# Writing the PSUM banks down per task and moving twenty-one tasks in a planned attention and Hyena kernel

## The chip, the cores and the metric

The kernel runs on one core of one Trainium2 chip. The metric is the device time of one execution in microseconds. The kernel before was timed in three runs: 375.69, 372.85 and 372.73 us, a median of 372.85 us. The profile shows one further execution, whose instructions span 370.8 us.

## The reference

The program computes an attention with an extra one in the denominator of the softmax, and feeds it to a gated long convolution:

```python
scores = scale * q @ k.T                      # 8 batches, 12 heads, 448 x 448, head size 64
e = np.exp(scores - m)                        # m: the row maximum
attn = e / (e.sum(-1) + np.exp(-m) + 1e-9)
x = (attn @ v)                                # gathered to 8 x 448 x 768
proj = x @ w_proj                             # 768 -> x1, x2, x3 of 768 each
x2_conv = irfft(rfft(x2, axis=1) * rfft(filter, axis=0), axis=1)
out = (x1 * x2_conv * x3) @ w_out
```

Everything is float32 at the edges; the kernel works in bf16 between them and accumulates in float32.

## The kernel before

**Two parts.** `attention(i)` (L934) handles one pair of heads, i = 0 to 47, six to a batch. `dense(b)` (L1099) handles the projection, the convolution as matrix products and the output product of batch b, 0 to 7. Attention of a later batch is interleaved with the dense part of an earlier one, so that TensorE (PE) has dense matmuls to run while ScalarE (ACT) works through the exponentials.

**Tasks.** No engine's order is left to a compiler. Each step is handed to `Plan.add` (L83) as a task: its engine, an assumed cost, what it needs, what it makes, which buffers it takes and gives back. `Plan.run` (L91) walks through the tasks in a planned time of its own and emits them. Since `plan.ORDER` (L455) is filled, each engine runs its tasks strictly in the order of that list's numbers: an engine looks only at the first task of its queue (L227) and waits for it. `plan.FLIP` (L456) lists the tasks that run on the other of two engines, ACT or VectorE (DVE), than the one they are written with.

**PSUM.** Eight banks are shared by three kinds of tile: pairs of banks for scores (`sc`) and for attention outputs (`op`), single banks (`hy`) for everything else. `spots` (L171) hands them out while the plan runs: to each tile a bank that is free at that planned time, by rules of preference. A tile's first matmul therefore waits on the chip for whoever empties the previous tile of the same bank.

The tasks that this document speaks of, by the names used here:

- S(i, t): four score matmuls of head pair i into an `sc` pair, 64x64 tiles of the array (L947, L952); then an exponential on ACT (L966).
- ER(i): the part of `e @ v` from the short rest of the rows, 64x64 tiles, 16 matmuls (L977); a pair of head pairs shares one `op` pair of banks, and the even one's ER is the first to write it. V(i, u): the main part, 12 matmuls of 128x128 (L997). Then `norm` on DVE, three instructions (L1010 to L1012), gives the `op` pair back.
- G(b, dt, part): six matmuls of the gate projections (L1273). Part 0 is copied to `x1` (L486 on ACT or L488 on DVE); part 1 is multiplied with it into `g` on DVE (L1288).
- PS(b, dt): six matmuls of the convolved projection (L1175), copied to a staging tile (L486 or L488), then turned by a DMA transpose into `x2` (`turn2`, L1188). Z(b, ...) are the matmuls on `x2` (L1223).
- I(b, dt): four matmuls back from the spectrum (L1319), copied to `cr`, added and subtracted into `cw` (L1335, L1337) and `cv` (L1346), multiplied with `g` into `y` (L1361: `yT` and, for the last 64 rows, `yR`).
- O(b, st, ch): the output product from `y` (L1091); the first three of a batch come as four matmuls and then two. It is copied into `osb`, of which there are three (L394), and stored by SP (L1406). A copy into `osb` waits until the store that used the buffer three before has landed.
- Loads: SP issues loads of q and k (L727, L747), of the rests (L509) and the DMA transposes into `qT`, `kT` (L694, L705), `xT` (L1056) and `x2` (L1188). GpSimd (POOL) issues the loads of v (L754) and casts q, k, v and the rests (L733, L759, L771, L514). Both run in their own fixed order.

Of the kernel before, what the change touches and what calls it, by code (L numbers as in the profile page):

```python
# [41 lines left out]
class Plan:  # L42
# [17 lines left out]
    FLIP = ()  # L60
    FETCH = (4.6, 256, 150)
# [14 lines left out]
    def __init__(self, rings):  # L76
        self.size = rings
        self.tasks = []
        self.banks = {}
        self.kept = []  # L80
        self.open = []

    def add(self, eng, cost, want, emit, need=(), make=(), take=(), give=(), dma=0.0, run=256, n=1, after=0.0, begun=(), late=0.0, turn=False, part=None, keep=False, port=False, mode=None, alt=None, mm=None):  # L83
        if alt:
            own = (eng, cost)
            (eng, cost), alt = (alt, own) if len(self.tasks) in self.FLIP else (own, alt)
            emit = lambda f=emit, e=eng: f(e)
        want = self.ORDER[len(self.tasks)] if self.ORDER else want + self.SHIFT.get(part, 0.0)
        self.tasks.append((want, len(self.tasks), eng, cost, emit, need, make, take, give, dma, after, run, n, begun, late, turn, keep, port or eng == "POOL" and not dma, mode or ("full" if eng == "PE" and not keep else None), alt, 2 * (mm or max(1, round(cost / 0.17)) if eng == "PE" and cost else 0)))

    def run(self):  # L91
# [79 lines left out]
        def spots(t):  # L171

            found, count = {}, {}
            for r, tok in t[7]:
                if r not in self.CAP or (r, tok) in self.banks:
                    continue
                count[r] = count.get(r, 0) + 1
                have = sum(1 for o in self.banks if o[0] == r and gone.get(o, 1e9) > now + 1e-9)
                if have + count[r] > self.CAP[r]:
                    return None  # L180
                busy = {i for got in found.values() for i in got}
                open_ = [i for i in range(self.NBANKS) if i not in busy and until[i] <= now + 1e-9]
                if r in self.PAIRS:
                    pairs = [(max(until[i], until[i + 1]), i) for i in open_ if i % 2 == 0 and i + 1 in open_]
                    if not pairs:
                        return None
                    i = min(pairs)[1]
                    found[(r, tok)] = (i, i + 1)
                else:
                    if not open_:  # L190
                        return None
                    found[(r, tok)] = (min(open_, key=lambda i: (self.MATE and i ^ 1 in open_, i < self.LOW, until[i], i)),)
            return found

        def ready(t):
            e = t[2]
            if not self.ORDER and t[10] > now + 1e-9:
                return False
            for k in t[5]:
                if made.get(k, 0):  # L200
                    return False
                at, by = when.get(k, (0.0, e))
                if at + (self.LAT[by] if by != e else 0.0) > now + 1e-9:
                    return False
            if e in queues and t[9]:
                out = sum(h[2][12] for h in queues[e]) + sum(x > now + 1e-9 for x in landed[e])
                if out + t[12] > self.OPEN:
                    return False
            if spots(t) is None:
                return False  # L210
            new = {}
            for r, tok in t[7]:
                if (r, tok) in holds or r in self.CAP:
                    continue
                h = held[r]
                i = len(h) + new.get(r, 0) - self.size[r]
                new[r] = new.get(r, 0) + 1
                if i >= 0 and gone.get((r, h[i]), 1e9) > now + 1e-9:
                    return False
            return True  # L220

        while any(queue.values()):
            moved = False
            for e in queue:
# [9 lines left out]
                for key, at in spots(t).items():  # L234
                    self.banks[key] = at
                    for j in at:
                        until[j] = 1e9
# [9 lines left out]
                if t[20]:  # L247
                    after, block, shift = self.FETCH
                    wait, cost = 0.0, end - now
                    edge = (fed - shift) // block * block + block + shift  # L250
                    while edge <= fed + t[20]:
                        at = now + cost * (edge - fed) / t[20] + wait
# [35 lines left out]
        for i, (_, t) in enumerate(order):  # L288
            if i in full:
                self.fill(*full[i])  # L290
            if t[16]:
                mine = {x for key in t[8] for x in self.banks.get(key, ())}
# [46 lines left out]
def kernel(  # L339
# [101 lines left out]
    def couple(c):  # L441
# [6 lines left out]
    plan = Plan(  # L448
        {
            "e": NE, "er": 2 * NER, "k0": 2, "q0": 2, "u": 1, "w": 1, "xf": 1,  # L450
            "x2": 1, "x2s": 1, "x2h": 1, "xs": 2, "t0": 2, "t1": 2, "yh": 1, "g": 1, "x1": 2, "cr": 2, "cw": 1, "cv": 2, "yT": 1, "yR": 1,
            "os": 3,
        }
    )
# [61 lines left out]
    def staged(b):  # L516
# [3 lines left out]
        for hp in range(NHP):  # L520
# [6 lines left out]
            for n, (name, x, at, size) in enumerate(parts):  # L527
# [29 lines left out]
                if alone:  # L557
                    add("ACT" if first else "SP", 0.52 if first else 0.5, -21.0 if first else want + 0.1 * n, load,
                        make=[("s" + name, g)], after=hold, dma=0.95 if name == "q" else 0.71, run=50)
                elif hp % 2 == 0:  # L560
                    need = [("cv", g - 6), ("cv", g - 5)] if name == "v" and c >= 3 else []
                    if name != "v" and c >= 4:
                        need = [("c" + w, c - 4) for w in "kq"]
                    add("POOL", 0.73, want + 0.1 * n, load, need=need, make=[(made, g), (made, g + 1)], after=hold, dma=1.05 if name == "q" else 1.0, run=45)
                if hp == 0 and name != "q":
                    add("SP", 2.6, want + (0.05 if name == "k" else SLOT[0] + 0.05) if b == 0 else want - RE1 + 0.1 * n,
                        lambda name=name: rests_load(name, b),
                        need=[("cr" + name, b - 1)] if b else (), make=[("r" + name, b)],
                        dma=1.25, run=22, begun=[("ir", b)], n=4)
# [1055 lines left out]
    with (  # L1625
# [6 lines left out]
        for b in range(n_batches):  # L1632
            W["yT", b], W["yR", b // 2] = y, yr
            stable(b)
            plan = Plan(plan.size)
# [9 lines left out]
    with tc.manual_schedule(engines={E.PE, E.Pool, E.DVE, E.Activation, E.SP}):  # L1645
        plan = main
# [31 lines left out]
```

## Time and profile before

| | us |
|---|---|
| three timed runs | 375.69, 372.85, 372.73 |
| median of the runs | 372.85 |
| profiled execution, first to last instruction | 370.8 |
| median less that span | 2.05 |
| PE busy in the span | 356.4 (96%) |
| DVE busy | 274.8 (74%) |
| ACT busy | 237.5 (64%) |
| POOL busy | 127.6 (34%) |

The profiled execution has no timed total of its own, only its span; the 2.05 us between the span and the median are what lies around the instructions. A row of the timeline reads: start in us, length in us, engine, source line, operation, output and inputs, shapes, count, and in brackets how long the engine had been idle before it and what ended that. Matmuls overlap each other, so the distance between two starts says what a group costs, and its length says a little more. PE's weight loads have an engine name of their own, PEld. Rows are matched with tasks by the order of each engine's instructions.

### The profile page before, as it was taken

Reading aid. Unit: us, or ns where it says so; the run is one execution under the profiler, and the core shown is the slowest. Engines: PE = TensorE matmul, PEld = TensorE weight load, DVE = VectorE, ACT = ScalarE, POOL = GpSimd, SP = SyncE. Lnnn points to the kernel's source line nnn. Section 1 sums busy time; section 2 is a strip of 40 time slices with the busy share of each in tenths; the row PEclk is TensorE's granted clock in tenths of the full one; section 3 lists DMA queues with packets and bytes.
Section 4 is the critical chain, followed back from the end, with each engine's and each line's share of the span. In section 5 each row is a group of like instructions: output and inputs, shape, how many; then the busy total and the mean of one; then the engine's idle time right before and its main releaser. Section 6 shows DMA issues by size and latency. Waiting matters only on the chain. (4 is left out here: it accounts for less than half of the span.)

```text
span 370.8 us, 10707 instructions
## 1 busy us (share of the span) xinstructions
PE 356.4 (96%) x4300; PEld 211.8 (57%) x4300; DVE 274.8 (74%) x674; ACT 237.5 (64%) x379; POOL 127.6 (34%) x278
## 2 busy tenths in 40 slices
PE   7989999999999979999999999999999999999995
PEld 7666675554555545565555646665565655555552
DVE  5468659982789726897579977689459898779970
ACT  4999876756767548567565657867776561334343
POOL 9984251444625274265537523313100100000000
PEclk9999999999999999999999999999999999999999
DMA  9999999988999999999998799995830074125035
GB/s 169 194 191 204 207 207 205 206 169 160 168 242 156 229 214 208 235 242 192 206 182 202 166 245 192 262 208 122 171 72 1 7 196 89 42 45 170 4 129 172
DMA packets 133958, 61.93 MB, mean 167 GB/s; under 512 B 105165, under 2 KB 130704, under 8 KB 133904
## 3 DMA queue, kind: packets, MB, share of 16 engines
q1 hardware_dynamic: 111552, 48.71, 61.6%
q0 software_dynamic: 22112, 12.26, 25.4%
q8 instruction: 34, 0.56, 0.6%
q10 hardware_dynamic: 240, 0.23, 0.2%
q14 instruction: 20, 0.16, 0.2%
HBM read 43.86 MB, written 11.01 MB: 148 GB/s over the span
## 5 line engine op out<-in xcount | busy, mean ns | idle before, releaser
L966 ACT ACTIVATE e<-psum 128x896 bf16<-128x896 f32 x144 | 126.6, 920 | 40.8 <-PE psum L947 37.3
L1273 PE MATMUL psum<-xT,wproj_bf 128*128 128x448 bf16 x576 | 121.7, 353 | 0.1
L1273 PEld LDWEIGHTS <-wproj_bf 128*128 128x128 bf16 x576 | 53.4, 98 | 47.7 <-issue 5.0
L1091 PE MATMUL psum<-wout_bf,yT 128*128 128x384 bf16 x288 | 54.7, 326 | 0.8 <-DVE g L1288 0.4
L1175 PE MATMUL psum<-xf,wproj_bf 128*128 128x452 bf16 x252 | 53.9, 357 | 0.0
L947 PE MATMUL psum<-qT,kT 64*64 64x448 bf16 x576 | 45.4, 359 | 2.5 <-DVE g L1288 0.7
L997 PEld LDWEIGHTS <-e 128*128 128x128 bf16 x1152 | 42.0, 98 | 9.6 <-issue 5.2
L997 PE MATMUL psum<-vn,e 128*128 128x65 bf16 x1152 | 46.8, 194 | 0.0
L733 POOL CAST nat<-nat 112x512 bf16<-112x512 f32 x36 | 25.4, 708 | 44.7 <-DMA nat<-in_q_dram 41.8
L1241 DVE TENSOR_TENSOR t<-xs,hrs 113x768 bf16<-113x768 bf16 (+1 forms) x64 | 36.4, 578 | 2.9 <-ACT xs L486 2.3
L1288 DVE TENSOR_TENSOR g<-x,psum 128x448 bf16<-128x448 bf16 x48 | 29.2, 616 | 12.1 <-PE psum L1273 10.9
L1091 PEld LDWEIGHTS <-yT 128*128 128x128 bf16 x288 | 26.6, 98 | 19.9 <-issue 1.8
L1175 PEld LDWEIGHTS <-wproj_bf 128*128 128x128 bf16 x252 | 23.2, 96 | 22.2 <-issue 1.1
L486 ACT CAST x<-psum 128x448 bf16<-128x448 f32 (+1 forms) x39 | 20.4, 529 | 22.6 <-PE psum L1273 14.5
L759 POOL CAST nat<-nat 128x384 bf16<-128x384 f32 x36 | 21.5, 598 | 32.2 <-DMA nat<-in_k_dram 31.9
L486 ACT COPY osb<-psum 128x384 f32<-128x384 f32 x39 | 18.2, 486 | 20.1 <-PE psum L1091 15.9
L486 ACT CAST xs<-psum 113x384 bf16<-113x384 f32 (+1 forms) x41 | 19.2, 482 | 15.1 <-PE psum L1223 14.1
L1012 DVE TENSOR_TENSOR xb<-psum,den 128x896 bf16<-128x896 f32 x24 | 26.2, 1091 | 0.8
L486 ACT CAST cr<-psum 128x452 bf16<-128x452 f32 x35 | 18.0, 539 | 11.5 <-PE psum L1319 11.0
L947 PEld LDWEIGHTS <-kT 64*64 64x64 bf16 x576 | 15.6, 105 | 17.1 <-issue 12.9
L966 ACT ACTIVATE er<-psum 128x896 bf16<-128x896 f32 x24 | 22.2, 926 | 4.3 <-PE psum L952 3.5
L987 POOL MEMSET sinks<- 1x1 bf16 x18 | 1.6, 91 | 65.6 <-PE psum L977 65.6
(143 smaller groups left out, 501.3 us busy)
## 6 DMA issues: line engine op xcount, KB each, us to landing
nat<-in_q_dram SPq DMA_DIRECT2D x37, 224.0 KB, 3.8
out_dram<-osb SPq DMA_DIRECT2D x21, 384.0 KB, 3.5
nat<-in_k_dram SPq DMA_DIRECT2D x38, 192.0 KB, 3.9
nat<-in_v_dram POOLq DMA_DIRECT2D x15, 192.0 KB, 6.3
wproj_bf<-in_moe_w_proj_dram POOLq DMA_DIRECT2D x2, 1152.0 KB, 18.1
out_dram<-osb SPq DMA_DIRECT2D x12, 192.0 KB, 2.7
ks<-in_v_dram POOLq DMA_DIRECT2D x9, 192.0 KB, 4.9
rests<-in_k_dram SPq DMA_DIRECT2D x32, 48.0 KB, 4.3
```

The costliest lines, as they stand in the source:

```text
L486: nc.scalar.copy(to, of)
L733: lambda hp=hp, qsrc=qsrc: nc.gpsimd.tensor_copy(qn[:, hp].rearrange("p j (u d) -> p u j d", u=2), qsrc.rearrange("p (u j d) -> p u j d", ...
L759: lambda hp=hp, sv=sv: nc.gpsimd.tensor_copy(kn[:, hp // 2, 3 * (hp % 2) + 1 : 3 * (hp % 2) + 4].rearrange("p j (u d) -> p u j d", u=2), sv),
L947: nc.tensor.matmul(sc[r, u, 0:S], kT[b % 2][c, hp // 2, 3 * turned + t, r], qT[b % 2][c, hp, :])
L966: nc.scalar.activation(to, of, AF.Exp, scale=SCALE)
L997: nc.tensor.matmul(out_bank(u)[:, n + 3 * turned, :], P["e"][1 + t][:, o : o + 128], vn[b % 2][:, hp, 4 * u + t, :], start=False, stop=tur ...
L1012: nc.vector.tensor_tensor(W["xb", b][:, hp // 2].rearrange("p s (u d) -> p u s d", u=2), op[:, :, :, 0:DH], rec[:].unsqueeze(3).to_broadca ...
L1091: nc.tensor.matmul(ops[:n, :DCH], y[:, dt, 0:n], wout_bf[:, dt, ch * DCH : (ch + 1) * DCH], start=(dt == 0), stop=(dt == NDT - 1),)
L1175: nc.tensor.matmul(pps, wproj_bf[:, kt, D + dt * 128 : D + (dt + 1) * 128], W["xf", b][:, :, kt, 0:FQ], start=(kt == 0), stop=(kt == NDT - 1),
L1241: nc.vector.tensor_tensor(t[:K], L["xs", par, ch][:K], h, op=ALU.mult)
L1273: nc.tensor.matmul(p[:, :S], wproj_bf[:, kt, 2 * part * D + dt * 128 : 2 * part * D + (dt + 1) * 128], xT()[:, kt, 0:S], start=(kt == 0), ...
L1288: nc.vector.tensor_tensor(g[:, dt, :], L["x1", dt], p[:, :S], op=ALU.mult)
```

## The change

The planner gets a list `BANK`. The first time that a task takes a PSUM tile, the tile gets the next number of the list as its bank (or as the first bank of its pair), and `spots` may use no other:

```diff
+    BANK = ()
...
+        self.mine = {}
...
+        for r, tok in take:
+            if r in self.CAP and self.BANK:
+                self.mine.setdefault((r, tok), self.BANK[len(self.mine)])
...
-                if r in self.PAIRS:
+                mine = self.mine.get((r, tok))
+                if mine is not None:
+                    at = (mine, mine + 1) if r in self.PAIRS else (mine,)
+                    if any(i not in open_ for i in at):
+                        return None
+                    found[(r, tok)] = at
+                elif r in self.PAIRS:
...
-    plan.ORDER = (9, 0, 6, 1370, 8, 10, 1, 5, 13, 18, 20,
...
+    plan.ORDER = (9, 2, 6, 1370, 8, 10, 1, 5, 13, 18, 20,
...
+    plan.BANK = (4, 4, 6, 4, 4, 6, 5, 4, 4, 7, 5, 4, 5, 4,
...
```

The list has 535 numbers, one for each tile. Tile by tile they are the banks that the planner hands out in the kernel before. So no tile changes its bank; what the list does is to hold the banks where they are while tasks move.

`ORDER` is written anew, and many of its 2033 numbers differ, but read engine by engine only eighteen tasks stand elsewhere in their queue. From `FLIP` the tasks 1027 and 1573 go and 1635 comes in, which puts three copies on ACT instead of DVE. These are the twenty-one:

| engine | task | moved | now ahead of |
|---|---|---|---|
| PE | V(6, 0) | 1 earlier | the first four matmuls of G(0, 0, 0) |
| PE | V(17, 0) and V(17, 1) | 2 earlier each | S(18, 1), S(18, 2) |
| PE | G(2, 2, 0) | 8 earlier | S(20, 0), S(21, 1), the ends of O(1, 1, 0) and O(1, 0, 1), PS(2, 2), S(21, 2), S(21, 3), ER(20) |
| PE | V(26, 0) | 2 earlier | both parts of O(2, 1, 0) |
| DVE | `ft` scaling (L870) | 1 earlier | the cast of the first q |
| DVE | `g` of G(0, 3, 1) | 3 earlier | `cw`, `cw`, `cv` of the first pair of I |
| DVE | `y` of batch 0, first third | 8 earlier | among others a `norm` |
| DVE | a minimum of denominators (L1046) | 12 later | nothing; it waits longer |
| DVE | a sum into `yh`, batch 1 (L1247) | 3 earlier | `g` of G(1, 1, 1) and two others |
| DVE | `g` of G(1, 5, 1) | 1 earlier | the second `cw` of batch 1 |
| DVE | `yR` of batch 1, second third | 2 earlier | another `yR` and the `norm` of 18, 19 |
| DVE | `g` of G(2, 0, 1) | 1 earlier | the `norm` of 18, 19 |
| SP | transpose into kT(16) | 2 earlier | that of qT(16), a load of q |
| SP | transpose into kT(17) | 2 earlier | that of qT(17), the first `x2` of batch 1 |
| SP | load of k(23) | 2 earlier | loads of k(22), q(22) |
| POOL | half of the key rests of batch 4 (L514) | 7 earlier | casts of q(24), k(25), q(25), k(26), k(24), the issue of a load of v(26), v(27), the other half |
| POOL | cast of k(26) | 3 later | nothing |
| DVE to ACT | `x1` of G(0, 2, 0) | | |
| DVE to ACT | `cr` of I(4, 2) | | |
| DVE to ACT | staging copy of PS(5, 1) | | |

(Positions of DVE count without the copies that leave it.) No instruction is added or taken away, apart from single filler matmuls on zeros (L1566) that the planner puts into gaps of the first 40 us and whose number it works out anew.

More of the change, by code (lines that the diff above doesn't have):

```diff
@@ new lines @@
+    plan.BANK = (4, 4, 6, 4, 4, 6, 5, 4, 4, 7, 5, 4, 5, 4, 5, 5, 4, 1, 0, 5, 4, 0, 4, 1, 6, 2, 0, 2, 6, 0, 2, 0, 0, 6, 6, 6, 2, 4, 2, 2, 6, 0, 4, 4, 4, 6, 0, 0, 0, 2, 4, 0, 6, 2, 6, 2, 2, 6, 2, 0, 6, 0, 0, 4, 6, 6, 4, 0, 2, 0, 2, 4, 6, 6, 0, 2, 2, 2, 4, 0, 6, 6, 6, 0, 0, 0, 0, 4, 0, 4, 6, 4, 4, 6, 2, 4, 4, 6, 6, 6, 0, 6, 2, 4, 0, 4, 6, 4, 4, 2, 2, 4, 6, 0, 4, 0, 4, 0, 2, 2, 6, 4, 2, 4, 4, 4, 0, 4, 6, 2, 2, 0, 0, 4, 2, 2, 0, 4, 2, 6, 4, 6, 6, 2, 4, 2, 4, 2, 6, 2, 0, 2, 6, 4, 6, 4, 0, 4, 2, 2, 4, 0, 2, 6, 2, 6, 0, 4, 2, 6, 0, 0, 2, 6, 0, 4, 0, 6, 4, 4, 4, 6, 6, 4, 2, 2, 0, 0, 6, 0, 4, 6, 4, 4, 2, 6, 0, 2, 2, 6, 0, 6, 0, 4, 4, 4, 2, 2, 0, 0, 6, 2, 0, 2, 6, 2, 2, 6, 0, 6, 7, 6, 1, 0, 3, 2, 5, 3, 2, 4, 4, 4, 7, 5, 2, 3, 5, 1, 4, 0, 4, 5, 1, 4, 5, 4, 0, 5, 1, 0, 2, 4, 4, 5, 5, 3, 4, 6, 2, 2, 3, 3, 2, 2, 3, 2, 3, 4, 2, 3, 0, 1, 5, 7, 3, 2, 0, 1, 3, 7, 0, 1, 1, 6, 0, 2, 6, 7, 6, 7, 3, 2, 3, 7, 6, 6, 4, 0, 0, 1, 3, 7, 3, 7, 2, 0, 1, 1, 3, 0, 2, 1, 0, 3, 2, 7, 7, 1, 4, 1, 0, 4, 7, 4, 6, 6, 1, 2, 6, 5, 5, 1, 6, 2, 5, 0, 1, 4, 4, 7, 5, 0, 5, 3, 4, 4, 5, 7, 0, 7, 0, 1, 6, 0, 3, 1, 2, 3, 7, 5, 0, 4, 1, 2, 1, 4, 3, 0, 0, 2, 3, 4, 1, 3, 6, 7, 0, 2, 0, 1, 5, 3, 6, 5, 4, 7, 0, 7, 0, 0, 1, 1, 0, 7, 5, 4, 0, 6, 1, 3, 6, 2, 2, 7, 6, 2, 2, 7, 3, 7, 3, 7, 5, 6, 6, 2, 0, 4, 5, 1, 0, 6, 2, 1, 0, 6, 4, 7, 6, 2, 1, 6, 7, 2, 4, 5, 0, 3, 3, 7, 6, 4, 7, 3, 5, 2, 7, 5, 7, 6, 1, 1, 4, 4, 6, 7, 2, 5, 4, 5, 4, 4, 4, 5, 5, 5, 4, 7, 6, 5, 4, 6, 5, 4, 4, 4, 6, 5, 6, 6, 7, 4, 5, 3, 0, 4, 7, 2, 4, 5, 4, 2, 6, 7, 7, 7, 5, 6, 5, 5, 4, 4, 7, 7, 0, 5, 7, 5, 6, 5, 7, 0, 5, 4, 4, 3, 6, 6, 5, 4, 5, 3, 1, 7, 6, 7, 6, 4, 5, 7, 7, 6, 7, 6, 4)
@@ new lines @@
+    plan.FLIP = (30, 49, 71, 87, 94, 98, 376, 378, 380, 438, 464, 971, 975, 977, 979, 985, 993, 1018, 1029, 1074, 1105, 1110, 1114, 1125, 1133, 1143, 1173, 1199, 1207, 1211, 1221, 1240, 1253, 1256, 1260, 1270, 1276, 1286, 1294, 1320, 1322, 1351, 1353, 1368, 1381, 1383, 1388, 1398, 1400, 1428, 1436, 1472, 1476, 1481, 1505, 1514, 1518, 1523, 1533, 1541, 1585, 1599, 1604, 1611, 1618, 1635, 1640, 1644, 1649, 1651, 1675, 1679, 1689, 1693, 1703, 1746, 1751, 1753, 1772, 1777, 1782, 1796, 1802, 1810, 1814, 1824, 1838, 1856, 1900, 1905, 1907, 1909, 1916, 1932, 1940, 1944, 1954, 1994)
```

3 lines of the change are left out of this document (1 added, 2 removed).

## The prediction

> **What bounds the kernel now.** I read the page first, then the table by stretches, then the timeline wherever PE stood still.
>
> ```profile
> span 370.8 us, 10707 instructions
> PE 356.4 (96%) x4300; PEld 211.8 (57%) x4300; DVE 274.8 (74%) x674; ACT 237.5 (64%) x379; POOL 127.6 (34%) x278
> PEclk9999999999999999999999999999999999999999
> 100.00:120.00 20.00, 18.72 (x257) 10.70 (x255) 18.46 (x45) 14.96 (x23) 8.23 (x19) 1.00 1.23 190
> 120.00:140.00 20.00, 17.47 (x207) 10.00 (x206) 10.54 (x26) 10.38 (x15) 10.60 (x23) 1.00 1.06 216
> 300.00:320.00 20.00, 20.00 (x190) 11.26 (x191) 16.39 (x44) 7.04 (x11) 0.09 (x1) 1.00 0.44 111
> ```
>
> PE is the bound, at full clock. It idles 370.8 - 356.4 = 14.4 us in all, and a change that adds and removes no matmul can win nothing but that. The idle time is not spread out: the stretch 120 to 140 alone holds 20 - 17.47 = 2.5 us, and late stretches such as 300 to 320 hold none. So each move is worth the idle time of PE that lies where the task now stands, as long as nothing later gives it back.
>
> The largest stop, and its cause, in the timeline around it and in the view of the tile `osb`:
>
> ```profile
> 123.62 0.76 POOL L754 DMA_DIRECT2D ks<-in_v_dram  x1
> 124.72 0.41 SPq L1406 DMA_DIRECT2D out_dram<-osb  x1
> 125.97 1.09 DVE L1012 TENSOR_TENSOR xb<-psum,den 128x896 bf16<-128x896 f32 x1
> 127.02 0.38 PE L952 MATMUL psum<-qT,kT 64*64 64x448 bf16 x4
> 127.23 0.36 PE L947 MATMUL psum<-qT,kT 64*64 64x448 bf16 x4
> 127.23 0.62 DVE L1288 TENSOR_TENSOR g<-x,psum 128x448 bf16<-128x448 bf16 x1
> 129.45 0.57 PE L947 MATMUL psum<-qT,kT 64*64 64x448 bf16 x8
> 131.66 1.02 DVE L488 COPY osb<-psum 128x384 f32<-128x384 f32 x2 [3.81 <-DMA out_dram<-osb]
> 132.27 0.19 PE L977 MATMUL psum<-vn,er 64*64 64x65 bf16 x1 [2.25 <-DVE osb L488]
> 132.98 1.31 PE L1273 MATMUL psum<-xT,wproj_bf 128*128 128x448 bf16 x6
> 134.13 0.54 PE L997 MATMUL psum<-vn,e 128*128 128x65 bf16 x12
> DMA to landing us min/median/max: 4.3/5.6/6.8
> ```
>
> Two output copies want `osb` buffers, and the store that still reads one of them, issued at 124.72, lands only at about 131.6 (6.8 us, the longer of the two stores in that view). Until then DVE stands, the two banks under the copies stay full, and ER(20), whose `op` pair is those banks, holds PE. Then comes G(2, 2, 0) at 132.98, which needs none of this.
>
> **The change part by part.** The list of banks first: it names the banks that the tiles have now, so alone it moves nothing, and I cost it at 0.
>
> *G(2, 2, 0) into the stop.* One gate costs 134.13 - 132.98 = 1.15 us of PE. It now runs at about 127, ahead of the score groups. Its bank is emptied by the `g` of G(2, 0, 1), which is moved ahead of the `norm` with it: 1.09 us of `norm` and its two small instructions no longer precede it, so it ends near 126.5, and G can start at 126.9 without waiting. Behind it S(20, 0) to S(21, 3) come 1.15 us later. Does that hurt? The scores cost 0.21 us a group (127.02 to 127.23), so the last would have ended at 129.45 + 0.42 = 129.87; now it ends at 131.0, still before the copies free ER(20) at 132.27. The exponentials behind them shift, but the stop has room. So the stop shrinks by the whole gate: **-1.15**. If the store lands when ER(20) is next anyway, the cover is gone and the move is worth 0. What stays of the stop: 132.98 - 129.87 - 0.23 (ER with its change of tile, below) - 1.15 = 1.73 us.
>
> *V(26, 0) ahead of O(2, 1, 0).*
>
> ```profile
> 176.82 1.33 PE L1175 MATMUL psum<-xf,wproj_bf 128*128 128x452 bf16 x6
> 178.52 1.14 PE L1091 MATMUL psum<-wout_bf,yT 128*128 128x384 bf16 x6 [0.36 <-DVE g L1288]
> 179.49 0.54 PE L997 MATMUL psum<-vn,e 128*128 128x65 bf16 x12
> 179.96 0.38 PE L947 MATMUL psum<-qT,kT 64*64 64x448 bf16 x4
> ```
>
> The output product waits for a bank that DVE empties. A group like the one at 176.82 takes about 1.15, so PE could have gone on near 178.0 and lost 0.5. V takes 179.96 - 179.49 = 0.47 less a change of tile of 0.09, that is 0.38, and its operands are long there: **-0.38**, 0 if DVE is on time.
>
> *Two copies to ACT, `cr` of I(4, 2) and the staging copy of PS(5, 1).*
>
> ```profile
> 254.05 0.63 DVE L488 CAST nat<-psum 128x452 bf16<-128x452 f32 x1
> 255.21 0.92 ACT L966 ACTIVATE e<-psum 128x896 bf16<-128x896 f32 x1 [1.31 <-PE psum L947]
> 257.57 0.50 PE L1091 MATMUL psum<-wout_bf,yT 128*128 128x384 bf16 x2
> 258.66 0.62 DVE L1288 TENSOR_TENSOR g<-x,psum 128x448 bf16<-128x448 bf16 x1
> 258.78 0.30 PE L977 MATMUL psum<-vn,er 64*64 64x65 bf16 x14
> 259.33 0.38 PE L947 MATMUL psum<-qT,kT 64*64 64x448 bf16 x4 [0.25 <-DVE g L1288]
> ```
>
> DVE works without a pause up to the `g` at 258.66, whose bank the scores at 259.33 take. ER before them costs some 0.15, so 0.4 is lost there, and 0.15 more at 257.57. With the 0.63 of the copy at 254.05 off DVE, and the same again a little earlier, both go; ACT has 1.31 us free at 253.9. I take **-0.5**, between 0 and -0.55.
>
> *What lies ahead of 132 and does not count.* The other moves sit at or before the stop:
>
> ```profile
> 63.76 0.37 PE L1319 MATMUL psum<-bt,yh 113*128 113x113 bf16 x4 [0.41 <-DVE x L488]
> 76.86 0.82 PE L1091 MATMUL psum<-wout_bf,yT 128*128 128x384 bf16 x4 [0.31 <-DVE yT L1361]
> 102.98 0.53 PE L1223 MATMUL psum<-x,ft 113*113 113x384 bf16 x2 [0.81 <-DMA x<-ldm]
> 115.91 0.38 PE L947 MATMUL psum<-qT,kT 64*64 64x448 bf16 x4 [0.47 <-DVE g L1288]
> ```
>
> `x1` of G(0, 2, 0) on ACT frees the bank that I(0, 1) waits for (0.41); `y` and `g` of batch 0 come earlier and end the wait at 76.86 (0.31 and some before it); the earlier `g` of G(1, 5, 1) ends that at 115.91 (0.47). The scaling of `ft`, the `yh` sum and V(6, 0) act the same way on smaller waits, the late minimum only yields its place. Together about 1.2 to 2. But behind them PE meets two DMA landings, at 102.98 and 132.27. If those hold their time, PE only arrives earlier and waits longer: **0**.
>
> V(17, 0) and V(17, 1) ahead of S(18, 1) part two runs of 64x64 tiles that touched, two changes of tile more.
>
> ```profile
> 112.26 0.36 PE L952 MATMUL psum<-qT,kT 64*64 64x448 bf16 x4
> 112.56 2.44 PE L1273 MATMUL psum<-xT,wproj_bf 128*128 128x448 bf16 x12
> ```
>
> From the start of the last score group to the next 128x128 matmul pass 0.30 instead of the 0.21 of a group: 0.09 a change, 0.18 for the pair, hidden in the stop at 132; without that cover, +0.18. The Trainium skill, TensorEngine Tiling (Array Packing), section Tiling Modes, says that a change of tiling mode drains TensorE, which speaks against this move; the trace agrees that it costs something, and if a drain cost a matmul's whole 0.36 us the pair would come to +0.7 and still lie under the stop.
>
> *The queues.* On SP three entries pass two others each and no entry is added. On POOL the key rests of batch 4 now wait, ahead of seven others, for transposes that read the same tile:
>
> ```profile
> 121.55 1.93 SPq L705 DMA_TRANSPOSE kT<-nat  x1
> 122.72 0.77 POOL L733 CAST nat<-nat 112x512 bf16<-112x512 f32 x1 [6.66 <-DMA nat<-in_q_dram]
> 131.88 0.50 POOL L514 CAST nat<-rests 64x384 bf16<-64x384 f32 x1
> 133.90 1.69 SPq L1188 DMA_TRANSPOSE x<-ldm  x1
> 143.77 0.65 PE L1223 MATMUL psum<-x,ft 113*113 113x384 bf16 x3
> q0 software_dynamic: 530, 0.20, 14.0%
> ```
>
> The cast of q(24) waits some 3 us longer (an estimate: the transpose at 121.55 with the 4 us or so that other DMAs take here), and the v load of 123.62 behind it goes out at about 127. The rest of POOL's list is bound by later landings and ends no later than 131.88 + 0.50. PE wants the first result that hangs on it, the `x2` at 133.90, only at 143.77. Cost **0**.
>
> Sum: -1.15 - 0.38 - 0.5 = -2.0. On the profile's own span that is 370.8 - 2.0 = 368.8; with the 2.05 us between span and median, 372.85 - 2.0 = **370.8 us**. The unknown term is the store's landing, x: every us that it moves moves the end as far, since PE works almost without pause behind it. Earlier it can win the 1.73 left of the stop; later it costs without limit, and 2 us is what separates the two ends of the landings above (4.3 and 6.8) roughly. I take 0, as the queue ahead of the store has the same entries.
>
> **The rivals.**
>
> *A: the store comes earlier.* The v load leaves the time before the landing. In the window 118 to 133 the POOL queue took 14.0% of the engines' time, 2.1 of 15 us. If half or more of this goes behind the store, x is -1 to -1.73: 369.1 to 369.8. Against it: the load still overlaps the last 4 us. The Trainium skill, DMA: Bandwidth & Descriptors, section Issuing engines are not separate DMA queues, says that DMAs of all issuers run on the same 16 engines and interleave. By that rule the load did delay the store. The trace agrees as far as it goes: the store needed 6.8 us while that load was under way, the other store of the view 4.3.
>
> *B: the gain is hidden.* Either the timed runs do not have the stop at 132 (then the gate wins nothing: -0.38 - 0.5 = -0.9, 372.0), or ACT, now with 0.54 us more in two places, delays exponentials: 372 to 373. For it: one profiled execution only. Against it: two timed runs agree within 0.12 us.
>
> *C: slower, the store comes later.* Place: the DVE copy at 131.66. Price: 1 us per us. It decides from 2.0 us later, beyond 133.6. For it: some of SP's entries ahead of the store change places, and a store's landing took anything from 4.3 to 6.8. Then 373 to 375; a stop of more than 5.7 us extra would be needed for 1%. Against it: the transposes are the same number, and none is bigger.
>
> *D: it does not do what it says.* The list holds the banks as they are; were one of the moved tiles to wait for a bank that the planner would have chosen otherwise, PE would show a new wait at 127 or 175. Near 372.9.
>
> **How the numbers follow.** Forecast, x within -1 and +0.7: 0.46. A: 0.14. B and D: 0.26. C: 0.14. The range reaches over A, the forecast, B and D and the first part of C: 368.9 to 373.3. A measurement of this kernel tells about 1% (3.7 us) from no change. Faster by that needs the whole of A, half of its chance: 0.07. Slower by that is the far third of C: 0.05. Within 1%: 0.88.
>
> **What would show it right or wrong.** Right: in the profile after, gate matmuls (L1273) stand just before the scores near 127, the wait of ER (L977) for the `osb` copy is 1 to 1.3 us instead of 2.25, no wait at 178 and 259, and the wait for `x` at 103 has grown or stayed. The forecast is wrong if ER(20) no longer waits at all (x is more negative), if the copy waits past 133, if G(2, 2, 0) waits for the `g` of G(2, 0, 1), or if a new wait for `kT`, `qT` or `x2` appears behind 140.

## The result and the profile after

| | kernel before | changed kernel | ratio, 95% interval |
|---|---|---|---|
| first measurement, nine runs each | 372.85 us | 369.53 us | 0.993 [0.9904, 0.9957] |
| again, later (35 and 12 runs) | 371.86 us | 370.84 us | 0.9972 [0.9947, 0.9998] |

Faster by 0.3 to 0.7%. Both intervals end below 1, the second one by a hair, and each is 0.5% wide, so the size is known only roughly. Ratios and intervals are formed from the undisturbed runs alone and are not quotients of the medians. The profiled execution of the first measurement took 371.87 us with a span of 370.0 us, the second longest of its nine runs; the other kernels' profiles below help to read it.

The page of the changed kernel: the span, busy times, the granted clock of PE, and the row of the DMA engines, each digit the busy share of a slice.

```profile
span 370.0 us, 10699 instructions
PE 356.5 (96%) x4299; PEld 211.9 (57%) x4299; DVE 272.7 (74%) x671; ACT 238.9 (65%) x382; POOL 128.9 (35%) x278
PEclk9999999999999999999999999999999999999999
DMA  9999999999999999999999799995930084125035
```

The last row matters as much as the first two. The same row of the kernel before, which the prediction left out:

```profile
DMA  9999999988999999999998799995830074125035
```

Up to some 250 us the 16 DMA engines are busy almost without pause too. Two streams run side by side, PE's and the transfers', and PE stands still where it gets ahead of the other. The table by stretches of the changed kernel (length, busy time of PE, PEld, DVE, ACT, POOL; clock, DMA share, GB/s):

```profile
120.00:140.00 20.00, 20.00 (x243) 11.16 (x242) 11.23 (x27) 12.93 (x19) 11.07 (x25) 1.00 1.15 215
160.00:180.00 20.00, 17.56 (x214) 9.70 (x212) 15.20 (x33) 10.23 (x18) 10.24 (x23) 1.00 1.09 202
```

The stretch 120 to 140 held 2.5 us of idle PE before and holds none now; 160 to 180 holds 2.4 us that the prediction did not have. The timeline of the changed kernel at the old stop:

```profile
123.27 0.41 SPq L1418 DMA_DIRECT2D out_dram<-osb  x1
124.96 0.50 POOL L526 CAST nat<-rests 64x384 bf16<-64x384 f32 x1 [8.72 <-DMA kT<-nat]
126.25 1.30 PE L1285 MATMUL psum<-xT,wproj_bf 128*128 128x448 bf16 x6
128.52 1.02 DVE L500 COPY osb<-psum 128x384 f32<-128x384 f32 x2 [1.90 <-PE psum L1103]
130.31 0.28 PE L989 MATMUL psum<-vn,er 64*64 64x65 bf16 x13
```

G(2, 2, 0) stands at 126.25 as predicted. But the copies into `osb` at 128.52 wait for PE's products, not for a store, and ER(20) at 130.31 waits for nothing. And the changed kernel's waits of PE:

```profile
PE psum L1187 <- ACT ldm L498: 1.6, 1, 1.6
PE psum L1235 <- DMA x<-ldm: 1.4, 1, 1.4
PE psum L989 <- POOL sinks L999: 0.8, 1, 0.8
PE psum L959 <- DMA qT<-nat: 0.5, 1, 0.5
```

The second is the old wait at 103. The other three are new and lie behind 140; the first, in the timeline, is a staging tile that an `x2` transpose still reads:

```profile
175.87 0.54 ACT L498 CAST ldm<-psum 128x452 bf16<-128x452 f32 x1 [2.99 <-DMA x<-ldm]
176.47 1.33 PE L1187 MATMUL psum<-xf,wproj_bf 128*128 128x452 bf16 x6 [1.59 <-ACT ldm L498]
```

So this execution won the whole stop and gave most of it back. Whether either belongs to the kernel is what the experiments ask.

### The profile page after: what moved, and what is told of

Same layout as the page of the kernel before. It is cut to its first block, busy times and chain, and to the rows that moved or that the text cites. A ratio compares the mean times of both kernels' runs of the same rounds, so it can differ in the third digit from the quotient of the medians.

```text
span 370.0 us, 10699 instructions
## 1 busy us (share of the span) xinstructions
PE 356.5 (96%) x4299; PEld 211.9 (57%) x4299; DVE 272.7 (74%) x671; ACT 238.9 (65%) x382; POOL 128.9 (35%) x278
## 5 line engine op out<-in xcount | busy, mean ns | idle before, releaser
L1253 DVE TENSOR_TENSOR t<-xs,hrs 113x768 bf16<-113x768 bf16 (+1 forms) x64 | 35.1, 559 | 3.3 <-ACT xs L498 2.7
L771 POOL CAST nat<-nat 128x384 bf16<-128x384 f32 x36 | 19.7, 550 | 25.6 <-DMA nat<-in_k_dram 25.4
L1259 DVE TENSOR_TENSOR yh<-t 113x384 bf16<-113x384 bf16 (+1 forms) x64 | 24.7, 402 | 0.6
```

The source lines that it names most:

```text
L1253: nc.vector.tensor_tensor(t[:K], L["xs", par, ch][:K], h, op=ALU.mult)
L1259: nc.vector.tensor_tensor(yh[:K, par, n, ch * DCH : (ch + 1) * DCH], t[:K, 0, :], t[:K, 1, :], op=(ALU.subtract, ALU.add)[n],)
```

## The experiments

The theory to begin with is rival A's: the load of v that now goes out behind the store made it late. Against it stand that SP's queue as a whole is earlier, and that the landing is one execution's chance. The four kernels of the first group were run beside the same runs of the kernel before (30 runs, median 372.32 us).

**The list of banks alone.**

```diff
+    plan.BANK = (4, 4, 6, 4, 4, 6, 5, 4, ...
```

> The kernel before with the list of banks alone, no task moved. All theories: the instructions are those of the kernel before, so the ratio is 1.000 within 0.3%, some 372.8 us. What it tells apart is the landing of the store issued near 124.7. Traffic theory (the v load that POOL issues at 123.6 shares the DMA engines with the store and makes it late): landing again 6 to 7 us after issue, copy into osb waits past 131, ER(20) waits about 2.2 us. Chance theory (landings scatter from one execution to the next, and the changed kernel was lucky): landing anywhere from 3.5 to 7 us after issue, and ER(20)'s wait anywhere from 0 to 2.3 us.

372.02 us, ratio 1.0006 [0.9976, 1.0036]. The instructions are those of the kernel before, so this is a second profile of it. Its timeline, and the landing of the same store in the view of `osb` (issue to landing):

```profile
105.32 0.82 PE L1235 MATMUL psum<-x,ft 113*113 113x384 bf16 x2 [2.00 <-DMA x<-ldm]
126.00 0.41 SPq L1418 DMA_DIRECT2D out_dram<-osb  x1
126.11 0.76 POOL L766 DMA_DIRECT2D ks<-in_v_dram  x1 [0.29 <-POOL nat L745]
132.13 1.02 DVE L500 COPY osb<-psum 128x384 f32<-128x384 f32 x2
133.92 0.28 PE L989 MATMUL psum<-vn,er 64*64 64x65 bf16 x13
```
```profile
DMA to landing us min/median/max: 3.7/3.7/3.7
```

The store lands 3.7 us after its issue, though the v load goes out 0.11 us behind it, and ER(20) waits for no copy. The stop of 2.25 us on which the prediction rests was in one execution. In the fourteen profiles of this study the store needed 3.7 to 4.2 us in thirteen (3.7 here, 4.2 in the longest, below) and 6.8 in the profile of before alone.

That profile is also the only one of the fourteen in which the load goes out ahead of the store, 1.10 us (123.62 and 124.72). The DMA queues show what follows. These are the packets, megabytes and share of the 16 engines' time from some 1 to 3 us behind the store's issue, 126 to 128 before and 127 to 129 with the banks alone; q0 is the queue of POOL's load, q1 that of SP, and packets overlap, so that a share can pass 100%:

```profile
q0 software_dynamic: 384, 0.15, 80.9%
q1 hardware_dynamic: 147, 0.12, 21.3%
```
```profile
q1 hardware_dynamic: 564, 0.74, 111.1%
```

Before, the load has most of the engines' time in this stretch; with the banks alone it has none yet. So the traffic theory fits the late landing of that one execution. What falls is that this order belongs to the kernel: in the eight other profiles without the POOL moves the load goes out 0.02 to 0.42 us behind the store. No run puts it ahead by intent, so its effect is seen once and not tested.

In the place of the stop at 132 stands a wait at 103, 2.00 us instead of 0.81.

**G(2, 2, 0) alone.**

```diff
 PE:  ... 
+  G(2, 2, 0)
   S(20, 0), ..., ER(20)
-  G(2, 2, 0)
 DVE: g of G(2, 0, 1) and the second third of yR ahead of the norm of 18, 19
```

> The kernel before with the bank list, G(2,2,0) ahead of S(20,0), and the DVE moves that free its bank (g of G(2,0,1) and the second third of yR of batch 1). No move on POOL or SP. Traffic theory: the store lands as late as before, G fills 1.15 us of the stop, ER(20) still waits about 1.1 us; time 1.15 us less, 371.7, ratio 0.997. Phase theory (the store is earlier since SP's queue as a whole runs 1.4 us ahead): same, 371.7, as SP is not moved. Chance theory: the timed runs have the stop only sometimes, ratio 0.998 to 1.000.

372.25 us, ratio 1.0000 [0.9968, 1.0032]. Nothing, as the chance theory has it.

**The POOL moves alone.**

```diff
 POOL:
+  half of the key rests of batch 4
   casts q(24), k(25), q(25), k(24), load of v(26), ...
-  half of the key rests of batch 4
```

> The kernel before with the bank list and the two POOL moves alone (half of the key rests of batch 4 ahead of seven others, the cast of k(26) three later). Traffic theory: the v load goes out near 126.5 instead of 123.6, the store issued near 124.7 lands within 4.5 us, the copy into osb no longer waits beyond 129.5, ER(20) waits under 0.5 us; time 2.0 to 2.3 us less, 370.7, ratio 0.994. Phase theory: the store lands 6 to 7 us after issue as before, ER(20) waits 2.2 us, ratio 1.000, 372.8 us. Chance theory: ratio 1.000 whatever the profile shows.

371.37 us, ratio 0.9993 [0.9962, 1.0023]. The v load goes out at 128.55, 2.72 us behind the store, and the store still needs 3.7 us, as with the load close behind it.

**The changed kernel without the POOL moves.**

```diff
 POOL:
-  half of the key rests of batch 4
   casts q(24), ...
+  half of the key rests of batch 4
```

> The changed kernel with the two POOL moves undone, all else as changed. Traffic theory: the v load is back at about 123, the store lands 6 to 7 us after its issue, ER(20) waits 1 us or more again; 0.7 to 1.5 us slower than the changed kernel, 370.2 to 371.0, ratio to the kernel before 0.995 to 0.997. Phase theory: as the changed kernel, 369.5, ratio 0.993, no wait of ER(20). Chance theory: ratio 0.993.

368.40 us in seven runs, ratio 0.9908 [0.9876, 0.9941]: not slower, and the lowest median of all. No gain of the moves on POOL is seen here, and they may cost. Since the stop at 132 is no longer the question, the wait at 103 is; the next group (before: 35 runs, 372.37 us) tells SP's moves from those on PE and DVE ahead of it.

**The three SP moves alone.**

```diff
 SP:
+  transpose into kT(16)
   transpose into qT(16), load of q(18)
-  transpose into kT(16)
...
+  transpose into kT(17)
   transpose into qT(17), first x2 of batch 1
-  transpose into kT(17)
...
+  load of k(23)
   loads of k(22), q(22)
-  load of k(23)
```

> The kernel before with the bank list and the three SP moves alone (transposes into kT(16) and kT(17) two earlier, load of k(23) two earlier). SP theory: kT(17) no longer stands between the two x2 transposes of batch 1, so SP issues the second one, which Z(1,1,1) waits for near 103, some 1.3 us earlier; that wait (2.0, 2.35 and 2.5 us in the three kernels without the SP moves) falls to about 1; time 1.3 to 2.3 less than the kernel before, 370.5, ratio 0.9945 to 0.9965. Head theory (PE and DVE moves ahead of 103 bring the staging copies earlier, and SP follows): SP issues the second x2 transpose when it did before, wait at 103 stays 2.0 to 2.5, ratio 1.000.

371.53 us, ratio 0.9985 [0.9961, 1.0009]. In its timeline PE does not wait at Z(1, 1, 1):

```profile
101.94 0.36 PE L959 MATMUL psum<-qT,kT 64*64 64x448 bf16 x4
102.41 0.53 PE L1235 MATMUL psum<-x,ft 113*113 113x384 bf16 x2
```

But the time to landing of the second `x2` transpose, here and with the banks alone, says that the wait went another way than expected:

```profile
DMA to landing us min/median/max: 6.2/6.2/6.2
```
```profile
DMA to landing us min/median/max: 8.9/8.9/8.9
```

SP issues it at 96.13 here and at 96.40 there, 2.92 and 3.67 us ahead of the next group that PE runs on `x2` (99.05 and 100.07). So here it goes out later against PE, not earlier: the first `x2` transpose now stands behind kT(17). (In the kernels with the moves ahead of 132 it does go out earlier, 3.25 to 4.26 us ahead of that group in the five with kT(17) moved, 3.16 and 3.19 in the two without.) What is shorter is the time from issue to landing. It is 6.2 to 7.7 us in six of the seven profiles with kT(17) moved, and 8.8 in the changed kernel's first one; with kT(17) as it was it is 7.7 to 8.9 in the six profiles that show it. Why it is shorter is not shown.

**The changed kernel without the SP moves**, the diff above reversed.

> The changed kernel with the three SP moves undone. SP theory: the wait for x near 103 is back at 2 us or more, 1.3 to 2 us slower than the changed kernel, 370.8 to 371.5, ratio to the kernel before 0.997 to 0.999. Head theory: as the changed kernel, ratio 0.993, wait at 103 about 1.4.

371.03 us, ratio 0.9967 [0.9942, 0.9993], and PE waits 1.64 us at 103: by the SP theory in the time, a little short of it in the wait.

**The moves ahead of 132 alone**, without SP, POOL and G(2, 2, 0).

```diff
 PE:   V(6, 0), V(17, 0), V(17, 1) earlier
 DVE:  seven of the eight moves
 FLIP: x1 of G(0, 2, 0) on ACT
```

> The kernel before with the bank list and only the PE, DVE and ACT moves ahead of 132 (V(6,0), V(17,0) and V(17,1), the eight DVE moves without the g of G(2,0,1), the copy x1 of G(0,2,0) on ACT). SP theory: PE reaches 103 about 0.5 us earlier and waits there as much longer, 2.5 to 3 us; ratio 1.000, 372.3 us. Head theory: the x2 transposes go out 1 to 1.3 us earlier, wait at 103 stays near 1.4 to 2, time 1 to 1.5 less, ratio 0.996 to 0.997.

371.94 us, ratio 0.9997 [0.9965, 1.0028]. Its timeline:

```profile
104.34 0.53 PE L1235 MATMUL psum<-x,ft 113*113 113x384 bf16 x2 [2.51 <-DMA x<-ldm]
105.84 2.44 PE L1285 MATMUL psum<-xT,wproj_bf 128*128 128x448 bf16 x12
109.81 1.31 PE L1285 MATMUL psum<-xT,wproj_bf 128*128 128x448 bf16 x6
129.19 0.38 PE L959 MATMUL psum<-qT,kT 64*64 64x448 bf16 x4 [0.87 <-DVE xb L1024]
```

PE comes earlier and waits longer, as the prediction said of these moves: 2.51 us, against 2.00 to 2.47 in the three kernels above that have neither these moves nor SP's.

**The three late moves alone.**

```diff
 PE:   V(26, 0) ahead of O(2, 1, 0)
 FLIP: cr of I(4, 2) and the staging copy of PS(5, 1) on ACT
```

> The kernel before with the bank list, V(26,0) ahead of O(2,1,0) and the two copies on ACT (cr of I(4,2), staging copy of PS(5,1)) alone. By the prediction's terms 0.38 and 0.5 us less: 371.4, ratio 0.9976, and PE without a wait near 178 and 259. If PE is bound by landings there too (the x2 transposes behind 140 or later), ratio 1.000 and those waits come back elsewhere.

371.36 us, ratio 0.9975 [0.9948, 1.0001], 0.93 us less by the ratio, where 0.9976 was expected; the interval just includes 1. Its timeline:

```profile
178.45 1.33 PE L1187 MATMUL psum<-xf,wproj_bf 128*128 128x452 bf16 x6
179.62 0.54 PE L1009 MATMUL psum<-vn,e 128*128 128x65 bf16 x12
180.00 1.14 PE L1103 MATMUL psum<-wout_bf,yT 128*128 128x384 bf16 x6
181.06 0.38 PE L959 MATMUL psum<-qT,kT 64*64 64x448 bf16 x4
```

From PS to the scores pass 181.06 - 178.45 = 2.61 us instead of 179.96 - 176.82 = 3.14, and no wait is left there or near 259.

The last group (before: 35 runs, 371.86 us) asks what is steady in the changed kernel.

**The changed kernel again**, no edit.

> The changed kernel once more, for a second profile and beside the next three. If the waits behind 140 in its first profile (0.48 us for qT at 141.7, 0.85 for ER(25) at 161, 1.59 for PS(3,4) at 176.5) belong to the schedule, they stand here again, and the span is near 370. If they are one execution's landings, they are gone or elsewhere and the span is near 367.5, which is the median of its timed runs less 1.8. Ratio 0.993 either way.

370.84 us, ratio 0.9972 [0.9947, 0.9998]. Its profile has a span of 366.9 us, 3.1 less than the first one of the same instructions:

```profile
102.02 0.53 PE L1235 MATMUL psum<-x,ft 113*113 113x384 bf16 x2 [0.34 <-DMA x<-ldm]
126.69 1.29 PE L1285 MATMUL psum<-xT,wproj_bf 128*128 128x448 bf16 x6 [1.00 <-DVE g L1300]
173.75 1.33 PE L1187 MATMUL psum<-xf,wproj_bf 128*128 128x452 bf16 x6
174.92 0.54 PE L1009 MATMUL psum<-vn,e 128*128 128x65 bf16 x12
175.45 1.14 PE L1103 MATMUL psum<-wout_bf,yT 128*128 128x384 bf16 x6
176.51 0.38 PE L959 MATMUL psum<-qT,kT 64*64 64x448 bf16 x4
```

The three new waits behind 140 are gone: 0.48 + 0.85 + 1.59 = 2.9 us, nearly the whole difference of the spans. They come and go with the executions, and not in this kernel alone: the one at 161 stands in four other profiles (0.44 to 0.65 us), the one at 176 in two (0.52 and 1.06), the one for qT at 141.7 in one, the next kernel's (0.54). But G(2, 2, 0) waits 1.00 us for the `g` of G(2, 0, 1), which the prediction had named as a sign against itself.

**The changed kernel with G(2, 2, 0) back behind ER(20)**, the PE part of the second diff reversed.

> The changed kernel with G(2,2,0) back behind ER(20). Landing theory (the store lands some 4 us after its issue in nine of ten profiles so far, so ER(20) waits for no copy and there is no stop to fill): as the changed kernel, 369.5, ratio 0.993. Prediction's term (the stop is there in the typical execution): 1.15 us slower than the changed kernel, ratio 0.996, and ER(20) waits 1 us or more.

371.01 us, ratio 0.9987 [0.9957, 1.0018]; the intervals of this kernel and of the changed one beside it overlap for most of their length, so the times tell neither 0.993 nor 0.996. The profile does tell: ER(20) at 129.35 waits for no copy.

**The changed kernel without both, POOL moves and G(2, 2, 0).**

> The changed kernel without the two POOL moves and with G(2,2,0) back. POOL theory (the key rests hold POOL for 8.7 us, casts and v loads behind them go late, and PE waits between 141 and 177): faster than the changed kernel by 0.8 to 1.2, as the kernel without the POOL moves alone: 368.4, ratio 0.991. POOL moves worth nothing: 0.993. If G does fill a stop: 0.994 to 0.996.

371.00 us, ratio 0.9963 [0.9938, 0.9987], none of the three figures expected. Here the store needs longest of the thirteen, and PE has the wait that G's move replaces, for the `norm` of 18, 19:

```profile
127.13 0.38 PE L959 MATMUL psum<-qT,kT 64*64 64x448 bf16 x4 [1.08 <-DVE xb L1024]
```
```profile
DMA to landing us min/median/max: 4.2/4.2/4.2
```

Without the POOL moves the ratio is lower by 0.0022 with G moved (0.9908 against 0.993) and by 0.0024 with G back (0.9963 against 0.9987). Each is less than its uncertainty of about 0.004. Against the repeat's 0.9972 the first difference would be 0.0064, more than the uncertainty; the two measurements of the changed kernel leave this open.

**The transpose into kT(17) alone.**

```diff
 SP:
+  transpose into kT(17)
   transpose into qT(17), first x2 of batch 1
-  transpose into kT(17)
```

> The kernel before with the bank list and one move: the transpose into kT(17) two earlier on SP, so that it no longer stands between the two x2 transposes of batch 1. SP theory: this is the move that counts of the three; the second x2 transpose goes out as soon as its staging tiles are copied, the wait of Z(1,1,1) near 103 is under 1.4 us; ratio as the three SP moves together, 0.9985. If kT(16) or the load of k(23) did it: wait at 103 back to 2.0 to 2.5 us, ratio 1.000.

371.91 us, ratio 1.0008 [0.9979, 1.0038]. Its timeline:

```profile
102.56 0.53 PE L1235 MATMUL psum<-x,ft 113*113 113x384 bf16 x2 [0.22 <-DMA x<-ldm]
127.61 0.38 PE L959 MATMUL psum<-qT,kT 64*64 64x448 bf16 x4 [0.89 <-DVE xb L1024]
176.80 1.14 PE L1103 MATMUL psum<-wout_bf,yT 128*128 128x384 bf16 x6 [0.99 <-DVE g L1300]
```

The wait at 103 is as good as gone with this one move, but the expected 0.9985 is not there: PE meets waits for DVE at 127 and 177.

**All profiles in one table.** The start of one and the same group of PE in a profile, less its start in the profile of before, changes over a stretch by what the kernel won (-) or lost there. An example, 98.92 and 108.24 before, 98.21 and 107.49 in the changed kernel's second profile:

```profile
98.92 0.53 PE L1223 MATMUL psum<-x,ft 113*113 113x384 bf16 x2
104.48 2.44 PE L1273 MATMUL psum<-xT,wproj_bf 128*128 128x448 bf16 x12
108.24 1.30 PE L1273 MATMUL psum<-xT,wproj_bf 128*128 128x448 bf16 x6
```
```profile
98.21 0.75 PE L1235 MATMUL psum<-x,ft 113*113 113x384 bf16 x2
107.49 1.31 PE L1285 MATMUL psum<-xT,wproj_bf 128*128 128x448 bf16 x6
```

The difference goes from about -0.5 (the group at 99.13, which the rows merge with its neighbour) to -0.75: -0.26 in this stretch.

| profile | to 29 | 29 to 99 | 99 to 108 | 108 to 125 | 125 to 137 | 137 to 224 | 224 to end |
|---|---|---|---|---|---|---|---|
| banks alone | +1.89 | -0.74 | +2.77 | -0.66 | -2.10 | +0.56 | 0.00 |
| G alone | +0.07 | +0.29 | +1.53 | -0.12 | -2.91 | +1.62 | 0.00 |
| POOL alone | -0.16 | +0.43 | +3.24 | -0.66 | -2.76 | +1.05 | -0.01 |
| late alone | +2.76 | -0.56 | +0.62 | +0.19 | -1.74 | -0.05 | -0.56 |
| ahead of 132 alone | +0.16 | -0.50 | +1.92 | -0.65 | -1.84 | +0.05 | 0.00 |
| changed without SP | -0.09 | -0.42 | +1.05 | -0.65 | -2.91 | +2.11 | -0.52 |
| SP alone | +0.09 | +0.03 | -0.32 | +0.68 | -2.39 | -0.01 | +0.32 |
| kT(17) alone | +0.16 | 0.00 | -0.59 | -0.26 | -1.83 | +1.81 | -0.01 |
| changed, first | -0.46 | -0.32 | +0.76 | -0.65 | -2.91 | +2.81 | -0.01 |
| changed, second | -0.37 | -0.12 | -0.26 | -0.65 | -1.68 | -0.26 | -0.56 |
| changed, G back | +0.15 | -0.10 | -0.03 | -0.65 | -2.77 | +1.09 | -0.56 |
| changed without POOL | +0.20 | -0.48 | +0.06 | -0.51 | -1.74 | -0.24 | -0.56 |
| without POOL, G back | -0.46 | -0.19 | -0.05 | -0.65 | -1.64 | -0.25 | -0.56 |

Read by columns: 125 to 137 is shorter than in the profile of before in every kernel, with G moved (1.68 to 2.91) and without (1.64 to 2.77) alike. From 99 to 108 the six kernels with kT(17) as it was lose 0.62 to 3.24, the seven with it moved -0.59 to +0.76. In two of the six, banks alone and POOL alone, some 1.6 us of the loss is a slow clock (last section). And -0.56 at the end is in five of the seven profiles with the two late flips, to the hundredth, and -0.52 in a sixth; the changed kernel's first profile wins as much near 258, but lost it before, with a wait of 0.34 us for `g` at 242.79.

## Why the prediction was right, and which steps failed

370.8 us was forecast, 2.0 less; the two measurements give 3.3 and 1.0 less by their medians. The size was right, the working only in part. Of the 2.0 us, 0.88 came from terms that held and 1.15 from one that is not there; what stands in its place is open, so that the size came out is partly luck. Three of the prediction's own signs of being wrong appeared: ER(20) waits for no copy, G(2, 2, 0) waits for `g` in the second profile, and a new wait for `qT` stands behind 140 in the first.

- **The bank list, 0:** right, 1.0006.
- **G(2, 2, 0), -1.15:** wrong. The step that failed is the first one, that the store's landing at 131.6 is the kernel's. The prediction quoted the two landings, 4.3 and 6.8 us, and took the longer for the rule. In thirteen of fourteen profiles the store needs 3.7 to 4.2 us and ER(20) waits for no copy. The first half of rival B was the truth for this term. Nor can G start without waiting each time: it waits for `g` 1.00 us in the second profile of the changed kernel and 0.94 without the POOL moves, and not at all in the three others with G moved. Where G stays, the scores behind the `norm` wait 0.33 to 1.08 us in six profiles and not in three.
- **V(26, 0), -0.38:** right at its place, where the profile of before had this wait. From PS to the scores the second profile of the changed kernel has 176.51 - 173.75 = 2.76 us instead of 3.14; by 192 some 0.11 of it is given back.
- **Two copies on ACT, -0.5:** right, at the upper end: 0 to -0.55 expected, -0.56 found. This term and the one before it were timed alone: 0.93 us less against 0.88, with an interval from 0 to 1.9 us, so that the profiles carry this and the time only agrees.
- **Ahead of 132, 0:** right for the moves on PE and DVE (0.9997, and the wait at 103 was 2.51 us). It was right for the reason given, that a landing follows, but only the landing at 103 does this. The two more tile changes of V(17) cost 0.21 us against 0.18: with the moves ahead of 132 alone 109.81 - 105.84 = 3.97 us pass from one gate group to the next, before 108.24 - 104.48 = 3.76. The stop that was to hide them is not there; the wait at 115.91 that went, 0.47, covers them.
- **The queues, 0:** the step that failed the other way, in the profiles. "If those hold their time" does not hold for the landing at 103: kT(17) no longer stands between the two `x2` transposes, and the wait is 0 to 1.36 us in seven profiles with that move, 1.43 to 2.51 in the six others and 0.81 in the profile of before. What goes with it is a quicker landing of the second transpose, more than an earlier issue. In the time it is not clear of zero: 0.9985 for the three moves alone, and 0.9967 for the change without them, which is slower than the 0.993 of the first measurement of the changed kernel, but not than the 0.9972 of the second. As the kT(17) kernel shows, later waits take most of it back.
- **Rival A** gave 369.1 to 369.8, where the first measurement lies, but not by its mechanism. It read the profile of before rightly: the load went ahead of the store there, and had most of the engines' time. But that was one execution in nine without the POOL moves; with the load 0.11 us behind it the store needs 3.7 us, and with the load 2.72 us behind it 3.7 us too. By this the POOL moves can win only what that rare order costs. The rule quoted there from the Trainium skill, DMA: Bandwidth & Descriptors, section Issuing engines are not separate DMA queues, that DMAs of all issuers interleave, agrees with the packets of before, where q0 and q1 share the engines in the same 2 us (80.9 and 21.3%).
- **Rivals C and D:** no later store, and no wait for a bank that the list would have caused.

The parts timed alone multiply to 1.0000 x 0.9993 x 0.9985 x 0.9997 x 0.9975 = 0.9950, between the two measurements of the whole. So no interplay has to be assumed, though factors that are each uncertain by 0.003 do not exclude one. Shown by the profiles are the late moves; that G finds no stop to fill; and that the wait at 103 is shorter with kT(17) moved. Open is how the other 0.1 to 1.7 us divide among SP's moves and those ahead of 132, and whether the POOL moves cost 0.8 us: 368.4 us without them was the lowest median, but the kernel that also has G back gave 371.0, so no better version is settled.

## What to carry to other kernels

A wait that ends on an engine's instruction is the better ground for a term: here -0.38 and -0.5 came back almost to the hundredth. It is no sure one. In the seven profiles of kernels without the late moves the wait at 259 was 0.25 or 0.26 us in six and 0.76 in one, the wait at 178 0.23 to 0.36 in four, 0.99 in one and 0 in two. A wait that ends on a DMA's landing is a poor ground, when the DMA row shows 9 everywhere; two profiles of the same instructions had it at 2.25 and at 0 us, so profile twice, by a neutral edit if need be, before a term rests on it. And where DMA is full beside PE, a moved entry of the DMA-issuing queue is not free: look which landing PE meets next, and what it meets after that.

## What the runs showed of the hardware

**The clock halved behind three of six stops of 2 us or more.** The banks-alone kernel behind its 2.00 us stop, and the G-alone kernel behind 2.35 us, by stretches (the clock is the third number from the right):

```profile
104.00:106.00 2.00, 0.68 (x3) 0.41 (x4) 0.00 (x0) 0.09 (x1) 0.76 (x3) 0.86 1.38 230
106.00:108.00 2.00, 2.00 (x28) 1.66 (x27) 1.72 (x4) 1.67 (x3) 1.33 (x4) 0.50 1.38 253
108.00:110.00 2.00, 2.00 (x10) 1.00 (x9) 1.69 (x5) 0.48 (x1) 0.02 (x1) 0.79 1.13 244
```
```profile
106.00:108.00 2.00, 2.00 (x22) 1.20 (x19) 1.90 (x6) 1.39 (x3) 0.48 (x2) 1.00 1.32 238
```

0.50 in the one, 1.00 in the other. POOL alone fell to 0.50 as well behind 2.47 us and the late moves alone behind 2.40 (near 8); ahead of 132 alone did not behind 2.51, nor did the kernel before behind 2.25. PE has no other wait of 2 us in the fourteen profiles, and nowhere else does its clock fall while it has matmuls to run. In the banks-alone profile the slow clock costs about 1.6 us more: its difference to before grows from 105.32 - 102.98 = 2.34 to 3.92 in the 5 us behind the stop. The timed runs agree: of 99 runs of the kernel before, the 20 with a mean granted clock below 0.997 took 373.3 us on average, the other 79 took 371.7. The Trainium skill, TensorE: Matmul & The Clock Gate, section HAM oscillation, warns of idle gaps beyond some 3.4 us; these traces show the fall behind a wait of 2.00 us, so here the measurement decides. That it comes in some executions only agrees with the free-running window of the same page's Part 1.

**The same program's executions differ by more than the change.** One program gave spans of 370.0 and 366.9 us, three waits behind 140 accounting for nearly all of it. The wait for `ft` at the start, 0.62 us before, was 1.73 us with the banks alone and 2.40 with the late moves alone; the first column of the table holds such differences, up to 2.76 us by 29 us.
